# A gated mix of a state-space model and an MLP: W1 sums made twice, a longer-running scan, full-size bias rows, another load order

## The chip, the cores and the metric

The kernel runs on one core of one Trainium2 chip. The time is that of the device in microseconds (us); smaller is better. Eight runs of the kernel before have a median of 574.28 us (573.9 to 575.57). Engines are named as the profile names them: PE multiplies matrices, PEld is its weight loader, DVE works on vectors, ACT applies functions, POOL and SP mostly issue transfers here.

## The reference

For `x` of 2048 rows by 1024 columns, all in bfloat16:

```
g = sigmoid((x * gate_w).sum(-1))
# a: state-space model, P = 1024 complex states
Bu = x @ B_bar.T                      # B_bar = ((Lam_bar-1)/Lam) * (B_re + 1j B_im)
h[t] = Lam_bar * h[t-1] + Bu[t]       # a scan over 2048 rows
a = 2 * Re(h @ C.T) + x * Dskip
# b: MLP
y = layernorm(x)
b = gelu(y @ w1 + b1) @ w2 + b2       # w1: 1024 x 3584, w2: 3584 x 1024
out = g * a + (1 - g) * b
```

## The kernel before, in words

**An order worked out ahead.** Every step is a task with an engine, a duration, a priority and the memory that it reads and writes (class `Graph`, L172). Before the program is written, `_schedule_once` (L225) plays the tasks through and fixes the order of each engine's instructions; `emit` (L347) then writes them out with a wait for each dependency on another engine. A low first number in a priority means early. At run time each engine takes its instructions strictly in this order, so a DVE or SP instruction that waits holds everything behind it on that engine. SP issues loads, POOL issues most stores.

**Products in seven parts.** All large products are done in groups that make four 128x512 result blocks from seven partial products instead of eight (class `SG`, L836; parts `p1` to `p7`). For this DVE makes sums and differences of operand blocks beforehand (`dve_tt`, L881). ACT copies intermediate PSUM banks (L846, L847, L854), and DVE or ACT evict the results. `mm` (L819) issues the 4 to 8 matmuls of one part, L828 those that start a bank and L830 those that add to it.

**Stages.** They follow each other on PE:

1. *Head, 0 to 26 us.* SP loads the first 128-row blocks of B (real, imaginary) and the first four of x. PE transposes them through PSUM (`t_x`, L641; `t_b`, L657); DVE copies x out, ACT copies B out. `tbank` gives PSUM banks 7 and 3 in turn. A transpose `cst_T` (L683) turns the small vectors into columns; a long chain of small DVE operations for the scan's tables starts from it.
2. *Projection `bu`, to about 124 us.* x times B. A narrow product (`z_gate`, L1024; into bank 7) gives for each row the gate's sum and the row sum for the layernorm. `z_move` (L1043) takes both through DRAM, once, after the second half. POOL and DVE make the layernorm; its result goes to DRAM and comes back transposed (`xn_load`, L1191).
3. *MLP, about 120 to 470 us.* Blocks of 1024 rows (c) and half of the 3584 hidden columns (Fh), in the order (Fh, c) = (0,0), (0,1), (1,1), (1,0). Each has an `m` part (times W1, GELU; seven groups) and a `b` part (times W2; four groups). `w1_prep` (L1219) brings one 256-column piece of W1 into one of four slots. On its first use the piece comes raw, DVE makes four sums from it (L1236 to L1239) and POOL stores piece and sums (`scr_w1`, L1241); on the second use this is loaded back (L1225). Each `b` group writes its result times (1-g) to DRAM (`scr_ac`), for Fh=1 by adding (L1366). For Fh=0, b2 is added by one more matmul in `p1` and in `p5`: its stationary operand is the first row, or the first two, of a constant tile `STG` (`v_one`, `v_sgn`, L690), its moving operand one or two rows of b2 in the region `B2B` (L1182, loaded at L1557).
4. *Scan, spread over stages 2 and 3.* Sixteen units (`ssm`, L1120): two groups of 512 states by eight pieces of 256 rows. Each loads from `scr_u`, does four wide products, four combinations, eight scans and a few small corrections on DVE (L1142 to L1173), and stores to `scr_h`. Its priority is 50, after that of the MLP's work (10). It has three slots in the region `SSM`, and its tables in `TABR`.
5. *Output `y`, about 470 to 567 us.* Eight groups, each for 256 rows: the state times C. `y_load` (L1417) loads the state (`H0`), the partial sums of the MLP (`AV`), x and the skip vector (`DB`), and DVE adds x * Dskip (`xd`, `xa`, L1433 and L1434, priority 52). The order of the row blocks is `YORD` (L1381). The arena regions of `H0`, `AV`, `XV`, `DB` are shared with the buffers of earlier stages, which decides when their loads can start. Before, the first two states lie in `SSM` and the first four partial sums in `TABR`: both become free when the scan is done. `y_load(0)` and `y_load(1)` stand before the last `b` group.

Of the kernel before, what the change touches and what calls it, by code (L numbers as in the profile page):

```python
# [419 lines left out]
def build(nc, A_x, A_Lambda_re, A_Lambda_im, A_B_re, A_B_im, A_C_re, A_C_im, A_log_dt, A_Dskip,  # L420
# [6 lines left out]
    CH = 512  # L427
# [18 lines left out]
    with es:  # L446
# [194 lines left out]
        def t_x(k, prio):  # L641
            bk = tbank()
            v = XNAT[k]

            def em(e, k=k, bk=bk):
                ins = None
                base = XNAT[k].ap
                for dt in range(DT):
                    src = AR.v(XOFF(k) + dt * 256, [(1, 128)]).ap
                    ins = e.transpose(V(PS16[bk], dt * 128, [(1, 128)]), src, V(IDENT, 0, [(1, 128)]))  # L650
                return ins
            g.add("pe", 0.06 * DT, prio, em, reads=[v, b_ident], writes=[b_ps[bk]], name="xT_T%d" % k)
            o = AR.v(xqo(0, 0) + k * 256, [(512, DT), (1, 128)])
            first_e.append(g.add("dve", 0.65, prio, lambda e: e.tensor_copy(o.ap, V(PS16[bk], 0, [(128, DT), (1, 128)])),
                                 reads=[b_ps[bk]], writes=[o, b_ps[bk]], name="xT_e%d" % k))

        def t_b(pt, prio):  # L657
            s = pt % 4
            for ri in range(2):
                bk = tbank()  # L660

                def em(e, ri=ri, bk=bk):
                    ins = None
                    for dt in range(DT):
                        src = AR.v(RX + s * 4096 + ri * 2048 + dt * 256, [(1, 128)]).ap
                        ins = e.transpose(V(PS16[bk], dt * 128, [(1, 128)]), src, V(IDENT, 0, [(1, 128)]))
                    return ins
                g.add("pe", 0.06 * DT, prio, em, reads=[BN[pt], b_ident], writes=[b_ps[bk]], name="bT%d.%d" % (pt, ri))
                o = AR.v(bqo(pt, 2 * ri), [(1, D)])
                first_a.append(g.add("act", c_act(D), prio, lambda e, o=o, bk=bk: e.activation(o.ap, V(PS16[bk], 0, [(1, D)]), AF.Copy),  # L670
                                     reads=[b_ps[bk]], writes=[o, b_ps[bk]], name="bTe%d.%d" % (pt, ri)))

        load_b(0, (-0.95, 0))
# [5 lines left out]
        for k in range(4):  # L679
            t_x(k, (-0.8, k))  # L680
        t_b(0, (-0.79, 0))
        bk0 = tbank()
        g.add("pe", 0.06, (-0.75, 0),  # L683
              lambda e: e.transpose(V(PS16[bk0], 0, [(1, NROW)]), V(STG, 0, [(1, 128)], npart=NROW), V(IDENT, 0, [(1, NROW)], npart=NROW)),
              reads=[b_stg, b_ident], writes=[b_ps[bk0]], name="cst_T", extra=[g.tasks[-2]])
        g.add("pool", 0.4, P0,
              lambda e: e.affine_select(V(STG, 0, [(1, 128)], npart=2), V(ONESF, 0, [(1, 128)], npart=2), [[0, 128]], ALU.is_equal, -1.0,
                                        base=0, channel_multiplier=1),
              reads=[b_ones], writes=[b_stg], name="signs").slack = 4.0
        v_one = View(V(STG, 0, [(1, 128)], npart=1), [b_stg])  # L690
        v_sgn = View(V(STG, 0, [(1, 128)], npart=2), [b_stg])
# [324 lines left out]
        b_zs = B("zs")  # L1016
# [26 lines left out]
        def z_move():  # L1043
            prio = (1.0, seq[0])

            def em_st(e):
                return [e.dma_start(out=ZS[r].rearrange("(c t) -> c t", c=NCH), in_=bass.AP(AR.h[F32], r * zrow + ZR // 4, [[32 * zrow, NCH], [1, CH]])) for r in range(2)]
            g.dma(prio, em_st, 2 * L * 4, sem("d_zst", True), reads=[zr], writes=[b_zs], name="zst", ndma=2, q="pool").slack = 0.5

            def em_ld(e):  # L1050
                return [e.dma_start(out=C(("Z", "SUM")[r], 0, NTT), in_=bass.AP(ZS.tensor, ZS.offset + r * L, [[1, 128], [128, NTT]]), allow_slow_non_contiguous=True) for r in range(2)]
            g.dma(prio, em_ld, 2 * L * 4, sem("d_zl"), reads=[b_zs], writes=[bc("Z%d" % k) for k in range(NTT)] + [bc("SUM%d" % k) for k in range(NTT)], name="zl", ndma=2)
# [15 lines left out]
        for c in range(2):  # L1068
            if c == 1:
                z_gate(0)  # L1070
            for pt in range(2):
                bu_plain(pt, c)
# [4 lines left out]
        for n, (pt, pr) in enumerate(order):  # L1077
            if pt not in summed:
                b_sums(pt, seq[0] - 1)
                summed.add(pt)  # L1080
            if (pt, pr) == (0, 1):
                z_gate(1)
                z_move()
                x_sums(1, seq[0])
            cur = bu_group(pt, pr)
            cur.p1()
            if prev is not None:
                prev.p7()
            cur.p5()
            cur.p6()  # L1090
            cur.p2()
            cur.p3()
            if prev is not None:
                prev.p4()
                opt = order[n - 1][0]
                if order[n - 1][1] == 1 and opt < 3:
                    bT_dma(opt + 5)
            prev = cur
# [21 lines left out]
        def ssm(pg, q):  # L1120
            s = nxt("sb", NSB)
            so, MA, MB = SB0 + s * 4096, TM0, TM0 + 4096
# [59 lines left out]
        v_b2l = AR.v(B2B, [(1, 512)], npart=1)  # L1182
        v_b2r = AR.v(B2B + 1024, [(1, 512)], npart=2)
# [35 lines left out]
        def w1_prep(j, first, q, ex=()):  # L1219
            s = nxt("w1", 4)  # L1220
            o0 = W1R + s * 7168
            w1slot[j] = o0
            if not first:
                o = AR.v(o0, [(1, 3584)])
                g.dma((10.0, q - 7), lambda e: e.dma_start(out=o.ap, in_=W1S[j]), 128 * 7168, ssem("w1", s), reads=[b_w1s[j]], writes=[o], name="w1l%d" % j, extra=ex)  # L1225
                return
            o = AR.v(o0, [(256, DT), (1, 256)])
            g.dma((10.0, q - 7), lambda e: e.dma_start(out=o.ap, in_=B_w1[:, j * 256:(j + 1) * 256].rearrange("(dt p) f -> p dt f", p=128)),
                  D * 256 * 2, ssem("w1", s), writes=[o], name="w1_%d" % j, bw=DMA_BW_512, extra=ex)

            def raw(fo, dh, dt=BF16):
                return AR.v(o0 + (dh * 1024 + fo * 128) * 2, [(256, 4), (1, 128)], dt)

            def sq(i):
                return AR.v(o0 + 4096 + i * 1024, [(128, 4), (1, 128)], FP16)
            dve_tt("w1a%d" % j, q, sq(0), raw(1, 0), raw(1, 1), ALU.add, 512)  # L1236
            dve_tt("w1b%d" % j, q, sq(1), sq(0), raw(0, 0), ALU.subtract, 512)
            dve_tt("w1c%d" % j, q, sq(2), raw(0, 0), raw(1, 0), ALU.subtract, 512)
            dve_tt("w1d%d" % j, q, raw(1, 0, FP16), raw(0, 1), sq(1), ALU.subtract, 512)  # L1239
            ov = AR.v(o0, [(1, 3584)])  # L1240
            g.dma((10.0, q), lambda e: e.dma_start(out=W1S[j], in_=ov.ap), 128 * 7168, ssem("w1s", s, True), reads=[ov], writes=[b_w1s[j]], name="w1s%d" % j, q="pool")  # L1241
# [85 lines left out]
        def b_group(Fh, c, tp):  # L1327
# [8 lines left out]
            if Fh == 0:  # L1336

                st["A11"], mv["B11"] = st["A11"] + [v_one], mv["B11"] + [v_b2l]
# [33 lines left out]
        H0 = [SSM, SSM + 8192] + [HT + 8192 * i for i in range(4)] + [SSM, SSM + 8192]  # L1372
        YR = HT + 49152
        AV = [TABR + 4096 * i for i in range(4)] + [YR + 4096 * i for i in range(4)]
        XV = [SSM + 16384, YR + 16384, YR + 18432, HT + 43008, HT + 45056]
        DB = SSM + 18432
# [4 lines left out]
        YORD = (4, 5, 6, 7, 0, 1, 2, 3)  # L1381
# [35 lines left out]
        def y_load(yi):  # L1417
# [3 lines left out]
            g.dma((52.0, yi), lambda e: e.dma_start(out=o.ap, in_=HS[qb]), 2 * UE * 128 * 2, ssem("hg", yi), reads=[b_hs[pg][qb] for pg in range(PG)], writes=[o], name="hg%d" % yi,  # L1421
                  extra=pe_last if yi > 2 else ())
            if yi == 0:
                g.dma((51.0, 0), lambda e: e.dma_start(out=v_db.ap, in_=bass.AP(A_Dskip.tensor, A_Dskip.offset, [[0, 128], [1, D]])), 128 * D * 2, sem("d_dskb"), writes=[v_db], name="dskb")
            for t in range(2):
# [3 lines left out]
                xi = 0 if n < 4 else 1 + n % 4  # L1429
# [3 lines left out]
                g.add("dve", c_tt16(D), (52.0, n), lambda e, xv=xv: e.tensor_tensor(xv.ap, xv.ap, v_db.ap, ALU.mult), reads=[xv, v_db], writes=[xv], name="xd%d" % k)  # L1433
                g.add("dve", c_dve(D), (52.0, n, 1), lambda e, xv=xv, av=av, k=k: e.scalar_tensor_tensor(av.ap, xv.ap, C("G", k), av.ap, ALU.mult, ALU.add),  # L1434
                      reads=[xv, av, bc("G")], writes=[av], name="xa%d" % k)

        def y_group(yi):
# [5 lines left out]
            su, s5 = AR.v(YU[yi % 2], [(1, 512)], F32), AR.v(AO + 16384, [(1, 512)], F32)  # L1443
# [23 lines left out]
        for (kind, Fh, c) in blocks:  # L1467
            if kind == "m":
                for j in range(NP2):
                    w1order.append((Fh * NP2 + j, (Fh, c) in ((0, 0), (1, 1))))  # L1470
# [37 lines left out]
        for n, it in enumerate(flat):  # L1508
# [4 lines left out]
            if (kind, Fh, c, x) == ("b", 1, 0, 3):  # L1513
                y_load(0)
                y_load(1)
# [39 lines left out]
            if n == 0:  # L1555
                def em_b2(e):
                    return [e.dma_start(out=AR.v(B2B, [(1, D)], npart=1).ap, in_=bass.AP(B_b2.tensor, B_b2.offset, [[0, 1], [1, D]])),  # L1557
                            e.dma_start(out=AR.v(B2B + 1024, [(1, 512)], npart=1, p0=1).ap, in_=bass.AP(B_b2.tensor, B_b2.offset, [[0, 1], [1, 512]]))]
                g.dma((40.0, 0), em_b2, 4096, sem("d_b2b"), writes=[v_b2l, v_b2r], name="b2b", ndma=2)
# [6 lines left out]
            if last_of_block:  # L1566
                if nit is None:
                    prev.p4()
                else:
# [13 lines left out]
                    else:  # L1583
# [5 lines left out]
                        prev.p4()  # L1589
                    prev = None  # L1590
# [53 lines left out]
```

## Time and profile before

| what | value |
|---|---|
| median of 8 runs | 574.28 us |
| the profiled execution's own time | 575.57 us |
| its span, first to last instruction | 573.8 us |
| mean granted TensorE clock | 0.998 |
| PE busy | 554.8 us, 2617 matmuls |
| DVE busy | 511.6 us, 865 instructions |
| ACT, POOL busy | 279.7 us, 99.5 us |
| moved by DMA | 134.5 MB, 234 GB/s |

All times are from one execution. In its lists a group of instructions has its line in the kernel, engine and operation, then the shapes of the operands and how often it ran. "Idle before" is the time in which the engine did nothing just ahead of an instruction, and the arrow names what ended this. Matmuls overlap in the records: one lasts 0.38 us, but the next starts 0.216 us after it.

### The profile page before, as it was taken

How to read it: one execution, taken by the hardware profiler on the slowest of the kernel's cores; microseconds unless marked ns; L12 is line 12 of the kernel's file. 1: busy time of each engine (PE TensorE's matmuls, PEld its weight loads, DVE VectorE, ACT ScalarE, POOL GpSimd, SP SyncE). 2: the span in 40 equal slices, each digit the busy share in tenths (PEclk: the TensorE clock that was granted, in tenths of full speed). 3: DMA queues.
4: the chain of work that ended last, by engine and by line, in shares of the span. 5: the costliest groups of instructions: out<-in, count | busy, mean ns of one | idle time of the engine just before them, and what ended most of it. 6: DMA issues, size and time to landing. Idle time of an engine off the chain costs nothing.

```text
span 573.8 us, 7480 instructions
## 1 busy us (share of the span) xinstructions
PE 554.8 (97%) x2617; PEld 249.3 (43%) x2617; DVE 511.6 (89%) x865; ACT 279.7 (49%) x465; POOL 99.5 (17%) x159
## 2 busy tenths in 40 slices
PE   4999999999999999999999999999999999999994
PEld 3444444444334444444434444444444444444442
DVE  2899899999999999999999999999995868998652
ACT  2978989666652247752226673236663322111110
POOL 0024766630101010001211000210000210011000
PEclk9999999999999999999999999999999999999999
DMA  9994999988994766413778998899569999777501
GB/s 269 246 276 99 285 268 295 339 282 268 368 282 121 257 243 224 157 37 111 254 293 295 342 322 181 210 278 265 186 145 244 318 304 287 245 245 271 174 37 55
DMA packets 116675, 134.50 MB, mean 234 GB/s; under 512 B 70548, under 2 KB 92565, under 8 KB 115614
## 3 DMA queue, kind: packets, MB, share of 16 engines
q1 hardware_dynamic: 102548, 79.72, 49.9%
q0 software_dynamic: 13952, 54.29, 29.1%
q8 instruction: 20, 0.33, 0.2%
q14 instruction: 17, 0.14, 0.1%
q10 hardware_dynamic: 138, 0.02, 0.0%
HBM read 63.48 MB, written 54.80 MB: 206 GB/s over the span
## 4 chain that ended last, share of the span: by engine, by line
PE 85%; DVE 9%; ACT 2%; issue 1%; DMA 1%; SPq 0%; DVEq 0%
PE ps L830 59%; PE ps L828 25%; DVE ar L882 3%; DVE ar L1142 2%; DVE ar L1275 2%; DVE ar L1156 1%; DVE ar L1145 1%; DMA ar<-in_A_x_dram 1%; ACT ar L670 1%; PE ps L1033 1%; PE ps L650 1%; DVE ar L1357 0%; ACT ar L912 0%; ACT L720 0%; ACT L1104 0%
## 5 line engine op out<-in xcount | busy, mean ns | idle before, releaser
L830 PE MATMUL ps<-ar 128*128 128x512 f16 (+1 forms) x1720 | 391.8, 379 | 2.2 <-DVE ar L1357 1.0
L830 PEld LDWEIGHTS ps<-ar 128*128 128x128 f16 (+1 forms) x1720 | 166.3, 98 | 207.4 <-issue 4.4
L828 PE MATMUL ps<-ar 128*128 128x512 bf16 (+1 forms) x752 | 183.7, 379 | 1.0 <-DVE ar L882 0.8
L882 DVE TENSOR_TENSOR ar<-ar 128x512 f16<-128x512 bf16 (+7 forms) x216 | 139.5, 683 | 8.1 <-PE ps L828 3.4
L828 PEld LDWEIGHTS ps<-ar 128*128 128x128 bf16 (+1 forms) x752 | 72.7, 98 | 90.1 <-DVE ar L882 3.5
L1156 DVE TENSOR_TENSOR_SCAN ar<-cst,init,ar 128x256 bf16<-128x256 f32 x128 | 87.8, 733 | 0.4
L846 ACT ACTIVATE ar<-ps 128x512 f32<-128x512 f32 x100 | 58.9, 593 | 48.1 <-PE ps L828 33.0
L1142 DVE TENSOR_TENSOR ar<-ar 128x2048 bf16<-128x2048 bf16 x64 | 77.1, 1216 | 0.0
L854 ACT ACTIVATE ps<-ps 128x512 f32<-128x512 f32 x66 | 38.5, 583 | 71.7 <-PE ps L828 71.5
L1271 ACT ACTIVATE ar<-ps,cst 128x512 bf16<-128x512 f32 x56 | 38.4, 687 | 25.7 <-PE ps L830 25.0
L847 ACT ACTIVATE ar<-ps,cst 128x512 f32<-128x512 f32 x32 | 22.0, 687 | 56.6 <-PE ps L828 35.7
L1354 ACT ACTIVATE ar<-ps,cst 128x512 f32<-128x512 f32 x32 | 22.0, 687 | 46.1 <-PE ps L830 46.1
L1277 ACT ACTIVATE ar<-ar,cst 128x512 bf16<-128x512 f32 x56 | 40.0, 715 | 8.9 <-DVE ar L1275 8.8
L1145 DVE TENSOR_TENSOR ar<-ar 128x1024 bf16<-128x1024 bf16 x64 | 42.2, 683 | 0.2
L1275 DVE TENSOR_TENSOR ar<-ps,ar 128x512 f32<-128x512 f32 x56 | 38.2, 682 | 2.8 <-PE ps L830 2.4
L897 POOL DMA_DIRECT2D scr_u<-ar x32 | 25.1, 786 | 52.1 <-ACT ar L912 17.8
L1357 DVE SCALAR_TENSOR_TENSOR ar<-ps,cst,ar 128x512 f32<-128x512 f32 x32 | 23.9, 746 | 11.2 <-PE ps L830 11.1
L1455 DVE SCALAR_TENSOR_TENSOR ar<-ps,cst,ar 128x512 bf16<-128x512 f32 x32 | 23.7, 746 | 9.7 <-PE ps L830 9.6
L1366 POOL DMA_DIRECT2D scr_ac<-ar x16 | 13.8, 881 | 81.2 <-issue 32.9
L1364 POOL DMA_DIRECT2D scr_ac<-ar x16 | 8.5, 534 | 100.6 <-DVE ar L882 47.7
L1462 POOL DMA_DIRECT2D out_dram<-ar x14 | 7.6, 546 | 83.4 <-DVE ar L1455 83.4
L1174 POOL DMA_DIRECT2D scr_h<-ar x16 | 9.6, 602 | 66.9 <-DVE ar L1145 66.7
(105 smaller groups left out, 262.0 us busy)
## 6 DMA issues: line engine op xcount, KB each, us to landing
scr_ac<-ar POOLq DMA_DIRECT2D x32, 512.0 KB, 7.6
scr_w<-ar POOLq DMA_DIRECT2D x14, 896.0 KB, 6.6
ar<-scr_w SPq DMA_DIRECT2D x14, 896.0 KB, 6.1
ar<-in_A_x_dram SPq DMA_DIRECT2D x32, 256.0 KB, 5.1
scr_u<-ar POOLq DMA_DIRECT2D x32, 256.0 KB, 5.0
ar<-scr_u SPq DMA_DIRECT2D x16, 512.0 KB, 5.9
scr_h<-ar POOLq DMA_DIRECT2D x16, 512.0 KB, 7.1
ar<-scr_ac SPq DMA_DIRECT2D x16, 512.0 KB, 7.4
```

The costliest lines, as they stand in the source:

```text
L828: ins = e.matmul(V(PS[bk], 0, [(1, n)]), st[i].ap, mv[i].ap, start=(i == 0), stop=(i == K - 1))
L830: ins = e.matmul(V(PS[bk], 0, [(1, n)]), st[i].ap, mv[i].ap, start=False, stop=(i == K - 1), skip_group_check=True)
L846: return e.activation(o.ap, V(PS[bk], 0, [(1, 512)]), AF.Copy)
L854: g.add("act", c_act(512), (pb[0], q - 2), lambda e: e.activation(V(PS[b], 0, [(1, 512)]), V(PS[a], 0, [(1, 512)]), AF.Copy), reads=[b_ps[ ...
L882: g.add("dve", c_tt16(n), (pb[0], q), lambda e: e.tensor_tensor(o.ap, a.ap, b.ap, op), reads=[a, b], writes=[o], name=nm, extra=ex).slack ...
L897: g.dma((1.0, q), lambda e: e.dma_start(out=US[pt // 4, :, 4 * pr:4 * pr + 4, r0:r0 + T], in_=evv.ap), 2 * 128 * CH * 2, ssem("us", 2 * ks ...
L1142: g.add("dve", c_tt16(UE), pri(i), lambda e: e.tensor_tensor(o.ap, a.ap, tbl.ap, ALU.mult), reads=[a, tbl], writes=[o], name=nm + tag)
L1145: g.add("dve", c_tt16(UE // 2), pri(i), lambda e: e.tensor_tensor(o.ap, a.ap, b.ap, op), reads=[a, b], writes=[o], name=nm + tag)
L1156: lambda e, pt=pt, ri=ri, vin=vin, go=go: e.tensor_tensor_scan(go.ap, Cb("R", pt, T), vin.ap, V(INIT, pt * 2 + ri, [(1, 1)]), ALU.mult, AL ...
L1271: g.add("act", c_act(512, ap_operands=1), (10.0, q + 1), lambda e: e.activation(o.ap, V(PS[bk], 0, [(1, 512)]), AF.Gelu_apprx_tanh, bias=C ...
L1275: g.add("dve", c_dve(512), (10.0, q - 2), lambda e: e.tensor_tensor(sv.ap, V(PS[bk], 0, [(1, 512)]), sv.ap, ALU.add), reads=[b_ps[bk], sv] ...
L1277: g.add("act", c_act(512, psum=False, ap_operands=1), (10.0, q + 3), lambda e: e.activation(o.ap, sv.ap, AF.Gelu_apprx_tanh, bias=C("B1", ...
```

## The change

- W1: both uses of the first half's seven pieces load them raw and make the four sums; they are not stored. The second half is as before.
- The scan gets a fourth slot: units 13 to 15 use slots 2 and 3 in turn, where slot 3 is `TABR + 4096`, in the first group's tables.
- Output stage: states, partial sums, x blocks and the skip vector have other places; the skip vector takes over `B2B`. The row blocks go in the order 4, 5, 6, 0, 1, 2, 3, 7. The loads for the first two groups, the first state aside, stand after the last `b` group. `xd` and `xa` have priority 49.
- b2: a POOL memset clears all 128 rows of `B2B`, the constant tile is filled over 128 rows, and the extra matmuls take 128-row operands.
- Head: x0, x1, B real, x2, x3, B imaginary are loaded and transposed in this order, through banks chosen by hand.
- The gate's sums go through DRAM in two halves.

The diff, cut:

```diff
-        load_b(0, (-0.95, 0))
+        def load_b0(ri, ap):
+            v = AR.v(RX + ri * 2048, [(1, D)])
+            g.dma((-0.9, 1.5 + 2 * ri), lambda e: e.dma_start(out=v.ap, in_=ap[0:128, :]), 128 * D * 2,
+                  sem("d_b0%d" % ri), writes=[v], name="bnat0.%d" % ri)
+
+        load_b0(0, A_B_re)
+        load_b0(1, A_B_im)
...
-        for k in range(4):
-            t_x(k, (-0.8, k))
-        t_b(0, (-0.79, 0))
-        bk0 = tbank()
+        t_x(0, (-0.8, 0), 7, [])
+        t_x(1, (-0.8, 1), 3, last_pe())
+        t_b(0, (-0.8, 2), (0,), (1, 2), last_pe())
+        t_x(2, (-0.8, 3), 0, last_pe())
+        t_x(3, (-0.8, 4), 7, last_pe())
+        t_b(0, (-0.79, 0), (1,), (1, 2), last_pe())
+        bk0 = 3
...
-              lambda e: e.affine_select(V(STG, 0, [(1, 128)], npart=2), V(ONESF, 0, [(1, 128)], npart=2), [[0, 128]], ALU.is_equal, -1.0,
+              lambda e: e.affine_select(V(STG, 0, [(1, 128)]), V(ONESF, 0, [(1, 128)]), [[0, 128]], ALU.is_equal, -1.0,
...
+                z_move(0)
...
-                z_move()
+                z_move(1)
...
-            s = nxt("sb", NSB)
-            so, MA, MB = SB0 + s * 4096, TM0, TM0 + 4096
+            un = pg * NQ + q
+            s = nxt("sb", NSB) if un < 13 else 2 + un % 2
+            so, MA, MB = (SB0 + s * 4096 if s < 3 else TABR + 4096), TM0, TM0 + 4096
...
-        v_b2l = AR.v(B2B, [(1, 512)], npart=1)
-        v_b2r = AR.v(B2B + 1024, [(1, 512)], npart=2)
+        v_b2l = AR.v(B2B, [(1, 512)])
+        v_b2r = AR.v(B2B + 1024, [(1, 512)])
+        v_b2 = AR.v(B2B, [(1, D)])
...
+            if j < NP2:
+                return
             ov = AR.v(o0, [(1, 3584)])
             g.dma((10.0, q), lambda e: e.dma_start(out=W1S[j], in_=ov.ap), 128 * 7168, ssem("w1s", s, True), reads=[ov], writes=[b_w1s[j]], name="w1s%d" % j, q="pool")
...
-                st["A11"], mv["B11"] = st["A11"] + [v_one], mv["B11"] + [v_b2l]
+                st["A11"], mv["B11"] = st["A11"] + [v_sgn], mv["B11"] + [v_b2l]
...
-        H0 = [SSM, SSM + 8192] + [HT + 8192 * i for i in range(4)] + [SSM, SSM + 8192]
+        H0 = [SSM] + [HT + 8192 * i for i in range(4)] + [SSM, HT, HT + 8192]
-        AV = [TABR + 4096 * i for i in range(4)] + [YR + 4096 * i for i in range(4)]
-        XV = [SSM + 16384, YR + 16384, YR + 18432, HT + 43008, HT + 45056]
-        DB = SSM + 18432
+        AV = [YR + 4096 * i for i in range(4)] + [AO + 2048, AO + 10240, TABR + 8192, TABR + 12288]
+        XV = [TABR, YR + 16384, YR + 18432, HT + 43008, HT + 45056]
+        DB = B2B
-        YORD = (4, 5, 6, 7, 0, 1, 2, 3)
+        YORD = (4, 5, 6, 0, 1, 2, 3, 7)
...
-                    w1order.append((Fh * NP2 + j, (Fh, c) in ((0, 0), (1, 1))))
+                    w1order.append((Fh * NP2 + j, (Fh, c) in ((0, 0), (0, 1), (1, 1))))
...
             if (kind, Fh, c, x) == ("b", 1, 0, 3):
-                y_load(0)
-                y_load(1)
+                y_load(0, ())
...
+                g.add("pool", 0.8, (39.0, 0), lambda e: e.memset(v_b2.ap, 0.0), writes=[v_b2], name="b2z")
                 g.dma((40.0, 0), em_b2, 4096, sem("d_b2b"), writes=[v_b2l, v_b2r], name="b2b", ndma=2)
...
+                        if nk == "y":
+                            y_load(0, (0, 1), False)
+                            y_load(1)
```

## The prediction

> **What bounds the kernel now.** I read first the page's busy table and slices, then the windows by stage, PE's waits, the chain that ended last, PE's and the weight loader's timelines around its gaps, then the built instruction order of both kernels.
>
> ```profile
> PE 554.8 (97%) x2617; PEld 249.3 (43%) x2617; DVE 511.6 (89%) x865; ACT 279.7 (49%) x465; POOL 99.5 (17%) x159
> ...
> PE   4999999999999999999999999999999999999994
> ...
> DVE  2899899999999999999999999999995868998652
> ```
>
> PE is the bound; DVE is as full until about slice 30 (430 us) and has air only after it. PE ends at 566.6: 6.8 us pass before its first instruction, 7.2 after its last, and 5.0 lie idle between (566.6 - 6.8 - 554.8). PE's timeline shows where:
>
> ```profile
> 6.77 3.71 PE L650 MATMUL ps<-ident,ar 128*128 128x128 bf16 x32 [6.77 <-DMA ar<-in_A_x_dram]
> ...
> 12.63 0.21 PE L684 MATMUL ps<-ident,stg 76*128 76x76 bf16 x1 [0.41 <-ACT ar L670]
> ...
> 24.00 1.89 PE L1033 MATMUL ps<-ar,gwc 128*2 128x512 bf16 x16 [1.43 <-DVE ar L768]
> ...
> 151.39 1.04 PE L828 MATMUL ps<-ar 128*128 128x512 f16 x4 [0.53 <-DVE ar L882]
> ...
> 299.18 4.28 PE L830 MATMUL ps<-ar 128*128 128x512 f16 x19 [1.02 <-DVE ar L1357]
> ```
>
> The bracket is idle time and what ended it. The other DVE waits over 0.2 are 0.23, 0.34, 0.23 and 0.31: 2.66 in all, at 145 to 161, 299, 324 to 331 and 430. There is also loss that no idle column shows. In the chain that ended last:
>
> ```profile
> 169.97 6.15 PE ps L830 x28
> 176.12 1.83 PE ps L828 x8
> ...
> 347.03 6.04 PE ps L830 x28
> ...
> 383.29 1.73 PE ps L828 x8
> ```
>
> The same 28 and 8 matmuls take 0.11 and 0.10 longer where a b2 row is mixed in (first W2 half) than where none is (second).
>
> **The change part by part.**
>
> *x first.* SP issues in order. Now B_re, B_im, x0 to x3; after: x0, x1, B_re, x2, x3, B_im, six transfers of the same size. So each slot keeps its landing and the tenants change. By the landing records the first two are in by 4.1, the others at 6.73, 7.27, 7.92, 8.59. Transposes of one block take 0.86 (1.71 for two). x0, x1 done by 5.8; B_re 6.75 to 7.6; x2 to 8.5; x3 to 9.35; B_im to 10.2; the constants' transpose 0.2. x3's copy (0.69) ends at 10.15, so the first projection matmul starts at about 10.4 instead of 12.67: **-2.3**. DVE's chain of constants starts after the same transpose, so DVE also gains 2.3. ACT's copies, which pace the chain from 14.6 to 21.5, follow B_im's, which moves by the same 2.2.
>
> *Bank rota.* The transposes of B alternate banks 7 and 3; six fixed banks at the head shift the rota by one. The gate matmul (bank 7) now waits for the copy of B block 3's real part (ended 22.46) and no longer its imaginary part (23.86). PE is done with transposes at 22.58, so the 1.43 gap closes: **-1.4**. Head for PE: **-3.7**.
>
> *b2 rows of full size.* Weight loader:
>
> ```profile
> 167.46 0.09 PEld L828 LDWEIGHTS ps<-ar,stg 1*128 1x128 bf16 x1 [0.42 <-issue]
> ...
> 169.58 0.09 PEld L828 LDWEIGHTS ps<-ar,stg 2*128 2x128 bf16 x1 [0.42 <-issue]
> ```
>
> The 1- and 2-row loads come late, and each costs 0.10 before and 0.11 after it. 16 x 0.21 = **-3.4** if a 128-row operand behaves as its neighbours. The Trainium skill, "TensorE: Matmul & The Clock Gate", LDWEIGHTS, speaks against it: loading time goes by columns, not by rows of the contraction; by that the sum has 0. The 0.09 here agrees with it about the load itself, but the spacing does not. "TensorEngine Tiling (Array Packing)", Key Properties, says that changing the array's tiling mode drains it, which would fit if one row counts as another mode; no record says so. I take the measured spacing, 3.4; the bounds are 0 and 3.4. New is a POOL memset of 128x1024 ahead of the two b2 loads on SP. The row near it (128x128, 205 ns) gives 0.2 to 1.6; I take 0.8. Behind it on SP is the first W2 quarter, issued at 130.1 when PE frees its place; the b2 loads went at 125.8, so 4 us cover it. On POOL, one store of u waits behind it; nobody needs that soon.
>
> *W1 sums twice.* Seven stores (0.55 each on POOL, 896 KB) and seven reloads go; seven raw loads of 512 KB come, and 28 sums:
>
> ```profile
> L882 DVE TENSOR_TENSOR ar<-ar 128x512 f16<-128x512 bf16 x66 | 26.1, 417 | 1.6 <-ACT ar L670 0.6 <-PE ps L828 0.5
> ```
>
> Back to back they are 0.34 to 0.41 apart: 28 x 0.357 = **+10.0 of DVE**, all in the stage 208 to 254, where DVE has 1.7 us free. It is hidden only by moving scan work out. The built order does: at the start of the second half's output block (345) 11.3 us less of the scan stands ahead on DVE than now. If that cover were gone, the 10 us would fall on PE. A W1 load is issued when a slot's matmuls end, two groups (12 us) ahead, and takes 6.4; SP waits ahead of these loads (a scan load behind a store of h, 7.1) end before PE frees the slot.
>
> *Gate sums moved in two halves.* Two more small stores on POOL (0.59 each, as the two now) and two more loads on SP. The first SP pair waits for its store and ACT's copy, at about 26; behind it stands a transpose of B that waits for PE until about 49 anyway. The layernorm chain starts earlier, PE never waited for it: 0.
>
> *DVE against PE.* At the sums that PE waited for (145 to 161 and 324 to 331), the new order has 0.3 to 3.1 us less DVE work ahead, mostly 0.65. That alone would end most of the 2.35 us of waits before 343. But PE, ahead by 3.7 + 3.4 + 2.35 = 9.45, would ask DVE to be 9.45 ahead too. DVE gets 2.3 from the head and 0.65 from the order: 2.95. The rest must come from its idle time, which between 26 and 343 is 9.8 us by the windows, for instance
>
> ```profile
> 168.00:208.00 40.00, 40.00 (x180) 17.03 (x181) 38.36 (x59) 12.00 (x18) 3.78 (x8) 1.00 0.61 191
> 254.00:294.00 40.00, 40.00 (x180) 16.90 (x179) 38.32 (x63) 12.05 (x18) 4.79 (x9) 1.00 0.55 191
> ```
>
> (third busy figure DVE.) These are short waits for PE's results (0.2 to 0.7), and shrink as PE runs ahead; but the order is fixed, and where both engines are full each waits sometimes. Gain by 343: 2.95 at worst, 9.45 at best; I take 3.55 of the 9.8, hence **-6.5**.
>
> *Scan into the output stage; y loads later.* DVE idles 14 us between 430 and 490, so the last scan unit, about 12.5 us, fits. The 0.31 at 430 goes (1.7 us less ahead): **-0.3**. y's partial sums now lie where W2 lay, and so do the second and third state: their loads start only as W2's last group frees them. From the second state's issue (457.8, PE's row) to the third's landing, 6.0 MB of loads and some 2.3 MB of partial-sum stores pass. These windows give the rate (last figures: DMA share, GB/s):
>
> ```profile
> 457.00:470.00 13.00, 13.00 (x62) 5.93 (x61) 10.42 (x15) 3.41 (x6) 2.58 (x3) 1.00 1.02 284
> 470.00:485.00 15.00, 15.00 (x71) 6.80 (x70) 10.75 (x14) 3.64 (x6) 1.43 (x2) 1.00 1.06 303
> ```
>
> 8.3 MB at 300 is 28 us: 485.5. It is needed at 493.2 (y2's sum, 0.7 ahead of PE at 493.9). x's block for y0's second row, issued at 468.4 behind a MB, lands at about 479 and must be there by 485.5 (3.2 us of DVE before PE's bank at 488.7). Six to eight us of cover; I charge **+0.3**. The order of blocks still ends with one whose outputs leave as now, so the 7.2 tail stays.
>
> Sum against the profiled execution: 573.8 - 6.5 - 0.3 + 0.3 = 567.3 span. That execution took 575.57, 1.8 more than its span; the median 574.28 is 0.5 more. Difference onto the median: **567.8**.
>
> **Rivals.**
> - *PE keeps it all:* DVE reclaims enough idle time: 574.3 - 9.75 = 564.5. For it: 9.8 us are idle. Against: they are spread over thirty-odd waits, some for ACT or POOL.
> - *DVE gives nothing back:* only its 2.95 passes, and 0.3: about 571.2. For it: DVE is 96 to 99% busy in most windows.
> - *Full-size rows gain nothing* (the page's rule holds): PE asks for 6.1; with DVE in between, some -5: 569.3.
> - *The output stage starves, slower:* the third state lands late. PE stalls if its 8.3 MB come below 234 GB/s (35.4 us), and the kernel is slower than before once the stall passes 6.5 us, below 198 GB/s. The window with the transposes of C, 427 to 440, ran at 195 (DMA share 0.95), and two of those transposes precede these loads on SP. Against: they are issued at 430, nearly 30 us earlier. Price 8 us: about 576.
>
> **How the numbers follow.** Forecast 0.46, PE keeps all 0.18, DVE holds 0.14, rows gain nothing 0.12, starved 0.10. The likeliest case has its own range of 565.8 to 570; for 8 in 10 I take 563.8 to 572.4, leaving out starvation and the edge of the best case. A change under 0.2% (1.15 us) cannot be told from none; a milder starvation would land there: faster 0.88, same 0.03, slower 0.09.
>
> **What would show it.** First projection matmul at 10.4 and no gap before the gate matmul; blocks with b2 at 6.04 and 1.73; 244 f16 sums of L882's kind in place of 216, with none of PE's waits in 208 to 254 over 0.3; PE's DVE waits in 145 to 331 under 1 us or DVE at 99%; DVE at 8 or more in slices 30 to 33; no PE wait for DVE at 470 to 495. I am wrong if the b2 spacing stays, if PE gains waits on DVE before 343 in place of the head's gain, or if the output stage shows waits for loads of h or of the partial sums.

## The result, and the profile after

Over 19 runs the changed kernel has a median of 572.2 us (567.15 to 580.97), the kernel before, over 56 runs, 575.24 us. The ratio is 0.9917, with a 95% interval of 0.9900 to 0.9935: faster by 0.8%, inside the predicted range of 563.8 to 572.4, but only 0.2 us inside its upper end and 4.4 us above the predicted 567.8. Five of the 19 runs lie at 567.15 to 568.04, at the predicted value. So the question is what the other runs lose. (Ratios leave out runs that are over 1.5% above the fastest of their kernel, while medians and ranges hold all; the profile of the changed kernel shown here is of such a run, 578.3 us with a span of 576.6.)

From the page of the changed kernel, busy times and slices:

```profile
PE 555.0 (96%) x2617; PEld 251.3 (44%) x2617; DVE 519.7 (90%) x893; ACT 279.4 (48%) x465; POOL 94.1 (16%) x155
...
PE   6999987899999999999999999999999999999995
...
DVE  4999885999999999999999999999998995999952
...
PEclk9999998899999999999999999999999999999998
```

DVE has 28 instructions and 8.1 us more (10.0 us were forecast), and fills slices 30 to 32 (counted from 0: 8, 9, 9 for 5, 8, 6), though not 33 (5 for 8). New are the holes of PE in slices 5 to 7, at 72 to 115 us, and of DVE in 5 and 6; the granted clock drops in slices 6 and 7. Line numbers differ between the kernels: L828, L830 and L882 of before are L839, L841 and L893 here, and others in the experiments. PE's timeline, the lines with the longer waits, with the idle time in brackets:

```profile
3.42 1.89 PE L649 MATMUL ps<-ident,ar 128*128 128x128 bf16 x16 [3.42 <-DMA ar<-in_A_x_dram]
6.11 1.03 PE L665 MATMUL ps<-ident,ar 128*128 128x128 bf16 x8 [0.80 <-DMA ar<-in_A_B_re_dram]
...
9.73 1.89 PE L839 MATMUL ps<-ar 128*128 128x512 bf16 x8 [0.28 <-DVE cst L704]
...
77.42 1.90 PE L841 MATMUL ps<-ar 128*128 128x512 bf16 x8 [2.02 <-ACT ar L857]
88.82 3.93 PE L841 MATMUL ps<-ar 128*128 128x512 f16 x16 [0.85 <-ACT ps L865]
97.81 3.52 PE L841 MATMUL ps<-ar 128*128 128x512 f16 x8 [2.47 <-ACT ps L865]
101.83 1.90 PE L841 MATMUL ps<-ar 128*128 128x512 bf16 x8 [0.51 <-ACT ar L857]
110.08 2.38 PE L841 MATMUL ps<-ar 128*128 128x512 bf16 x8 [2.03 <-ACT ar L857]
...
174.59 1.68 PE L839 MATMUL ps<-ar 128*128 128x512 f16 x7 [0.72 <-DVE ar L893]
...
302.65 4.28 PE L841 MATMUL ps<-ar 128*128 128x512 f16 x19 [0.38 <-DVE ar L1379]
```

The head came as forecast: the first projection matmul at 9.73 (forecast 10.4, before 12.67), and no gap ahead of the gate matmul. Then PE waits five times for ACT's copies of intermediate banks, where it never waited before. The waits between 55 and 125 us say what held ACT and DVE (the figures are total, times, longest):

```profile
DVE ar L893 <- DMA ar<-in_B_w_dram: 6.9, 1, 6.9
ACT ar L968 <- DMA scr_u<-ar: 5.1, 3, 2.8
PE ps L841 <- ACT ar L857: 4.6, 3, 2.0
...
DVE ar L893 <- DMA ar<-in_A_B_im_dram: 4.0, 2, 3.7
...
PE ps L841 <- ACT ps L865: 3.3, 2, 2.5
```

All are transfers: blocks of B that a DMA transposes, stores of u that give their buffers back, a piece of W1. None stands in this list of the kernel before.

The b2 rows did what was forecast. The chain that ended last has, for the first W2 half, the spacing that only the second had before (the first had 6.15 and 1.83), and the loader shows the 128-row operand like its neighbours:

```profile
176.49 6.04 PE ps L841 x28
182.53 1.73 PE ps L839 x8
```

```profile
169.18 1.39 PEld L839 LDWEIGHTS ps<-ar 128*128 128x128 bf16 x7
170.69 0.10 PEld L839 LDWEIGHTS ps<-ar,stg 128*128 128x128 bf16 x1
170.90 0.74 PEld L841 LDWEIGHTS ps<-ar 128*128 128x128 bf16 x4
```

To see where time goes, I compare the start of the same ACT or DVE instruction, one that follows PE directly, in two traces. This table gives the start minus that of the kernel before, in us; the head of the table has the time in the trace of before.

| kernel, own time of its profile | 26.0 gate copy | 67.7 u3 | 110.3 u7 | 160.7 GELU 6 | 339.0 GELU 13 | 463.9 last W2 | 508.0 y3 |
|---|---|---|---|---|---|---|---|
| changed, 578.3 | -4.25 | -4.26 | +7.76 | +6.48 | +3.03 | +2.98 | +3.12 |
| changed, again, 572.5 | -4.03 | -4.04 | -0.30 | +0.04 | -3.33 | -3.32 | -2.67 |
| b2 only, 573.45 | -1.19 | -1.01 | -1.13 | -0.92 | -3.69 | -3.62 | -2.12 |
| head only, 573.88 | -4.04 | -4.17 | -2.32 | -2.72 | -2.73 | -2.72 | -1.73 |
| head only, 584.39 | -4.89 | -5.02 | +8.97 | +8.55 | +8.55 | +8.56 | +8.76 |
| gate halves only, 585.5 | -1.09 | -1.06 | +6.00 | +10.19 | +9.82 | +9.89 | +9.86 |
| changed, gate in one piece, 571.0 | -3.39 | -3.48 | -3.39 | -4.34 | -6.06 | -5.93 | -4.24 |
| changed, old head, 586.6 | -1.07 | -1.00 | +11.60 | +15.04 | +11.10 | +11.22 | +11.50 |
| changed, old head, gate in one piece, 572.8 | -1.22 | -1.15 | -1.21 | -0.93 | -2.86 | -2.74 | -2.41 |
| changed, old head, stores held, 575.1 | -0.11 | -0.04 | +1.67 | +1.23 | -1.19 | -1.13 | -0.15 |
| changed, stores held, 572.6 | -3.34 | -3.35 | +0.26 | -1.43 | -3.09 | -2.97 | -2.85 |
| changed, W1 sums stored, 572.6 | -3.76 | -3.83 | -3.89 | -2.96 | -4.17 | -3.60 | -3.33 |
| b2 and W1, 596.5 | -0.72 | -0.65 | -0.71 | -0.35 | -3.17 | -2.92 | +21.36 |

The column at 67.7 is steady: -3.4 to -5.0 with the new head, 0 to -1.2 with the old one (the trace of before happened to get its first x late, at 6.77; with the old head the others start at 5.0 to 6.0). Most of the spread between the traces comes in by the next two columns, at 110.3 and 160.7; the other large loss is that of the last row, at the output.

### The profile page after: what moved, and what is told of

It is laid out like the page before. It is cut to its first block, busy times and chain, and to the rows that moved or that the text cites. A ratio compares the mean times of both kernels' runs of the same rounds, so it can differ in the third digit from the quotient of the medians.

```text
span 576.6 us, 7505 instructions
## 1 busy us (share of the span) xinstructions
PE 555.0 (96%) x2617; PEld 251.3 (44%) x2617; DVE 519.7 (90%) x893; ACT 279.4 (48%) x465; POOL 94.1 (16%) x155
## 4 chain that ended last, share of the span: by engine, by line
PE 79%; DMA 8%; DVE 8%; issue 2%; ACT 0%; SPq 0%; DVEq 0%; ACTq 0%
PE ps L841 54%; PE ps L839 24%; DMA ar<-in_B_w_dram 4%; DVE ar L893 3%; DMA ar<-in_A_B_im_dram 2%; DMA scr_u<-ar 2%; DVE ar L1297 1%; DVE ar L1160 1%; DMA ar<-in_A_B_re_dram 1%; PE ps L665 1%; PE ps L1044 1%; DVE ar L1163 0%; DVE ar L1174 0%; DVE ar L1019 0%; PE ps L649 0%
## 5 line engine op out<-in xcount | busy, mean ns | idle before, releaser
L841 PE MATMUL ps<-ar 128*128 128x512 f16 (+1 forms) x1720 | 394.7, 381 | 9.1 <-ACT ar L857 4.6
L841 PEld LDWEIGHTS ps<-ar 128*128 128x128 f16 (+1 forms) x1720 | 167.8, 98 | 216.9 <-ACT ar L857 7.8
L839 PE MATMUL ps<-ar 128*128 128x512 bf16 (+1 forms) x752 | 184.6, 380 | 1.5 <-DVE ar L893 1.2
L893 DVE TENSOR_TENSOR ar<-ar 128x512 f16<-128x512 bf16 (+7 forms) x244 | 150.7, 652 | 13.9 <-DMA ar<-in_B_w_dram 6.9
L839 PEld LDWEIGHTS ps<-ar 128*128 128x128 bf16 (+1 forms) x752 | 73.1, 98 | 91.5 <-DVE ar L893 3.7
L968 ACT ACTIVATE ar<-ps 128x512 bf16<-128x512 f32 x28 | 16.7, 596 | 10.4 <-DMA scr_u<-ar 5.1
```

Of the source, the lines that this page charges most:

```text
L839: ins = e.matmul(V(PS[bk], 0, [(1, n)]), st[i].ap, mv[i].ap, start=(i == 0), stop=(i == K - 1))
L841: ins = e.matmul(V(PS[bk], 0, [(1, n)]), st[i].ap, mv[i].ap, start=False, stop=(i == K - 1), skip_group_check=True)
L893: g.add("dve", c_tt16(n), (pb[0], q), lambda e: e.tensor_tensor(o.ap, a.ap, b.ap, op), reads=[a, b], writes=[o], name=nm, extra=ex).slack ...
```

## The experiments

Theory 1 was that the early head pushes transfers together at 60 to 115 us and loses its gain there. The rival was the gate part, which lets the layernorm, and so its stores, start earlier.

**The change again.**

> The changed kernel, unaltered, once more, because its profiled execution lost some 12 us between 75 and 115 us, where PE waited for ACT's copies, ACT for stores of u and DVE for W1 and for transposed blocks of B. Theory 1 (late transfers are an accident of an execution, not of the order): a profile of an undisturbed execution has under 1 us of PE waits between 60 and 120, keeps the head's 4.4 us there, and spans about 565.5. Theory 2 (the new order always collides there): waits of 5 us or more in the same place again, and a span over 570.

569.42 us (566.58 to 572.51, 6 runs), ratio 0.9895 [0.9858, 0.9933]. Its six runs fall into three at 566.6 to 567.7 and three at 571.2 to 572.5. The profile is of one of the latter. PE's waits between 60 and 120 us sum to 3.74, more than Theory 1's 1 us and less than Theory 2's 5, so neither theory holds as it stands. From PE's timeline:

```profile
78.51 1.90 PE L841 MATMUL ps<-ar 128*128 128x512 bf16 x8 [2.89 <-ACT ar L857]
103.71 1.90 PE L841 MATMUL ps<-ar 128*128 128x512 bf16 x8 [0.85 <-ACT ar L857]
127.78 3.63 PE L841 MATMUL ps<-ar 128*128 128x512 f16 x16 [1.45 <-ACT ps L865]
152.56 3.63 PE L841 MATMUL ps<-ar 128*128 128x512 f16 x16 [0.25 <-DVE ar L893]
168.23 1.69 PE L839 MATMUL ps<-ar 128*128 128x512 f16 x7 [0.72 <-DVE ar L893]
...
487.85 1.90 PE L839 MATMUL ps<-ar 128*128 128x512 bf16 x8 [0.55 <-DMA ar<-scr_h]
```

The wait at 78.5 comes after DVE stood 4.69 us for a transposed block of B. The one at 127.8 is of another kind: DVE has scan work ahead of the evictions there, and ACT waits 2.09 us for DVE. The last one, at the output, is for the third state.

**b2 rows alone.** The kernel before with

```diff
-                st["A11"], mv["B11"] = st["A11"] + [v_one], mv["B11"] + [v_b2l]
+                st["A11"], mv["B11"] = st["A11"] + [v_sgn], mv["B11"] + [v_b2l]
```

and the memset, the constant tile and the views of 128 rows.

> The kernel before with only the full-size b2 rows (memset, 128-row constant tile, 128-row operands). If the measured spacing is due to the 1- and 2-row operands: runs of 28 matmuls after a b2 row take 6.04 in place of 6.15, those of 8 take 1.73 in place of 1.83, and the span falls by up to 3.4 us, less what DVE takes back since its order is the old one: -1.5 to -3.4. If the rows' size does not matter: 0.

574.16 us (571.66 to 584.3, 22 runs), ratio 0.9974 [0.9957, 0.9991]. Between 160.7 and 339 the shift goes from -0.92 to -3.69, a gain of 2.8 where 16 operands at 0.20 would give 3.2. At the output 1.5 of it is lost again, in the old output stage. By the median the gain is 1.1 us, under the 1.5 to 3.4 that were expected.

**Head alone.** Loads, transposes and banks of the head on the kernel before.

```diff
-        load_b(0, (-0.95, 0))
+        load_b0(0, A_B_re)
+        load_b0(1, A_B_im)
...
-            t_x(k, (-0.8, k))
+        t_x(0, (-0.8, 0), 7, [])
+        t_x(1, (-0.8, 1), 3, last_pe())
```

> The kernel before with only the head's new order of loads, transposes and banks. By the prediction PE's first projection matmul starts 2.3 us earlier and the gate matmul 3.7 earlier; with DVE's order of the old kernel the time falls by 2 to 3.7 us. Theory: the earlier start alone brings on the late stores and transposes between 75 and 115 us; then its runs spread as those of the changed kernel do (6 us between lowest and upper quarter) and the median gains under 1 us. Rival: the spread has another cause; then all runs lie within 3 us and the gain stays.

582.62 us, from 573.88 to 595.13 over 22 runs; the kernel before on the same chip has 575.25. A head that is 3 us earlier makes the kernel 7 us longer in the median. Over the ten shortest runs alone the ratio is 1.0036 [1.0009, 1.0064]: still slower, by 2 us. The profile, of the best run, shows the head's 4.2 and a loss of 1.9 between 67.7 and 110.3, in which PE waits 1.62 us at 93.6.

**Gate in one piece.** The changed kernel with one store and one load of the gate's sums:

```diff
-                z_move(0)
...
-                z_move(1)
+                z_move()
```

> The changed kernel with the gate's sums moved in one piece after the second half, as before. If the earlier layernorm stores and the transposes that follow them cause the waits between 75 and 115 us: the runs draw together and the median falls by 2 to 5 us against the changed kernel, to about 567. If not: the same 572 with the same spread.

572.38 us (568.68 to 576.56, 19 runs), ratio 0.9939 [0.9916, 0.9962]. The expectation failed: the median didn't fall to 567, and the middle half of the runs spreads over 5.5 us, in the changed kernel over 5.9. Its best run (568.68) is even 1.5 to 2 us above the best runs of the changed kernel (567.15 and 566.58). So by the run times the gate halves cost the changed kernel nothing that can be told from zero. Its profile, of one run, is what the prediction forecast: no loss at 60 to 115, -6.06 at 339 (forecast -6.5). It then loses 1.8 at the output, in one wait:

```profile
484.55 1.90 PE L841 MATMUL ps<-ar 128*128 128x512 f16 x8 [1.60 <-DVE ar L1473]
```

DVE had stood 8.0 us for blocks of x in this stage. What makes this kernel's other runs up to 5.6 us longer than the profiled one was not profiled.

**Old head.** The changed kernel with the head of before.

> The change without its first part: x and B are loaded in the old order and the transposes keep the old banks, all else is as after the change. Theory 1 (the early head is what makes the transposed blocks of B and of the normalized x late between 60 and 115, so its gain comes back there): no waits of DVE on transposed B above 0.5 us, no waits of PE on copies of u, runs within 3 us of each other, and a time of 575.2 - 3.3 (b2 rows) - 2.4 (PE's waits for DVE before 343) - 0.3, or about 569.3, no slower than with the head. Theory 2 (the gate sums in halves do it, since they start the layernorm stores 6 us earlier, into the transposes): the lateness and the spread stay, with a time of 572 to 576. Theory 3 (the head is worth its 3.7 in the runs that go well): the best runs are 3 to 4 us above the best of the changed kernel (566.6).

587.4 us (586.57 to 588.6, 4 runs), ratio 1.022 [1.0186, 1.0255]: worse than the kernel before, and steadily so. Theory 1 as written falls: the early head isn't needed for the collision, the gate halves are enough. That is Theory 2, though the time goes far beyond its 572 to 576. SP's timeline shows it, here of before:

```profile
65.74 5.25 SPq L1062 DMA_TRANSPOSE ar<-in_A_B_im_dram  x2
74.52 5.05 SPq L1197 DMA_TRANSPOSE ar<-scr_xn  x2
```

and here with the old head and gate halves:

```profile
62.29 17.33 SPq L1065 DMA_TRANSPOSE ar<-in_A_B_im_dram  x2
79.80 9.02 SPq L1205 DMA_TRANSPOSE ar<-scr_xn  x2
```

Issuing the last two transposes of B takes 17.3 us in place of 5.3, and they land 23.6 and 14.0 us after their issue, before 7.3 and 5.9. The stores of normalized x left at 61.5 to 72.5 us, in the kernel before at 66 to 80. DVE waits, then ACT's copies, then PE:

```profile
DVE ar L881 <- DMA ar<-in_A_B_im_dram: 12.6, 1, 12.6
PE ps L829 <- ACT ar L845: 8.5, 2, 8.3
```

**Old head and gate in one piece.**

> The old head and the gate sums moved in one piece; b2 rows, W1 sums twice and the output stage as after the change. Theory 1: as the kernel before in its first 120 us, so neither lateness nor spread, about 569.3. Theory 2: the same here, and 3 us or more better than the run that has only the old head. If the gate halves are worth something by an earlier layernorm chain: slower than that run.

572.92 us (570.77 to 580.0, 10 runs), ratio 0.9964 [0.9936, 0.9992]. Taking the halves away is worth 14.5 us here. Its first 120 us are those of the kernel before. It stays 3.6 us above the 569.3 that Theory 1 expected: PE waits 1.26 us for ACT at 126.8, and 3.1 us for DVE in six places (before 2.7 in six).

**b2 and W1 twice, old output stage.**

```diff
-                    w1order.append((Fh * NP2 + j, (Fh, c) in ((0, 0), (1, 1))))
+                    w1order.append((Fh * NP2 + j, (Fh, c) in ((0, 0), (0, 1), (1, 1))))
...
+            if j < NP2:
+                return
```

> The kernel before with full-size b2 rows and the W1 sums made twice, with the old buffers and block order of the output stage. The built order still defers 8.5 us of scan past the second half's first sums (11.3 after the change). Theory (10.0 us more of DVE lie beside other work as long as scan can be deferred): within 1.5 us of b2 rows alone (574.2), with the two DVE waits at 145 to 161 smaller. Rival (the 10 us need the new output stage as their cover): PE waits for DVE between 343 and 495, and the time is 578 to 584.

596.08 us (593.74 to 596.6, 4 runs), ratio 1.0356 [1.0322, 1.0390]. The rival was right that the old output stage doesn't hide the 10 us, though the loss is larger than its 578 to 584, and PE waits for a load, not for DVE. Up to 464 nothing is lost (-2.92). But the scan ends at 458.5 where it ended at 430, and the state that lies in the scan's own memory can't be loaded before. SP's timeline of the loads of h, first of before, then of this run, and PE's timeline of this run:

```profile
442.14 16.08 SPq L1421 DMA_DIRECT2D ar<-scr_h  x2
```

```profile
476.58 0.33 SPq L1423 DMA_DIRECT2D ar<-scr_h  x1
```

```profile
457.74 7.72 PE L829 MATMUL ps<-ar 128*128 128x512 f16 x34
487.45 5.78 PE L827 MATMUL ps<-ar 128*128 128x512 bf16 x16 [21.99 <-DMA ar<-scr_h]
```

The last store of h goes out at 464.3, takes 12.3 us, and only then the load is issued. The kernel with the new places and block order (the run before this one; it differs from this in them, in the order and priority of the output stage's loads and sums, and in the scan's fourth slot) has 572.92. So this part of the change is worth 23 us to a kernel that makes the W1 sums twice.

**W1 sums stored.** The changed kernel with the first half's sums stored and loaded again.

> After the change, but the first half of W1's sums is stored and loaded again as before: 28 sums (10.0 us of DVE) fewer, seven stores and seven loads of 128 KB in place of seven loads of 512 KB. Theory (the second making is hidden): the same time as the whole change, 567 to 572, within 1 us at equal luck in the first 120 us. Rival (DVE, not PE, sets the pace up to 343): 2 to 5 us faster than the whole change, 563 to 567. Second rival (the stores and their reloads cost more than the sums): 1 to 3 us slower.

573.88 us (570.7 to 578.34, 10 runs), ratio 0.9975 [0.9945, 1.0004]. Ten us less for DVE make nothing faster: the second making is hidden. It is 1.7 slower than the changed kernel's median, as the second rival had it, but the ranges lie over each other. Head and gate halves are both in this kernel, and its profile shows no loss between 67.7 and 110.3 (-3.83 to -3.89): with both, the collision comes in some executions only.

**Stores held, old head.** If the stores of normalized x are what holds the transposes up, then holding the stores must undo it:

```diff
+                hold = [t for t in g.tasks if t.name == "bs4_%d" % (5 + c)] if c < 2 else []
...
-                      reads=[xv, bc("RSTD" + s), bc("NMR" + s)], writes=[o], name="ln_norm%d" % k)
+                      reads=[xv, bc("RSTD" + s), bc("NMR" + s)], writes=[o], name="ln_norm%d" % k, extra=hold)
```

> The run with the old head and the gate sums in halves (587.4), with one edit: the first four normalized blocks of x are made after the sums of transposed B block 5, the next four after those of block 6, so that their stores leave some 6 us later. Theory (stores of normalized x that leave while B's last blocks are being transposed hold those transposes up, and through them DVE, the copies and PE): DVE's wait of 12.6 us for B falls under 1 us, no wait of PE over 1 us between 60 and 115, and the time comes to that of the old head with the old gate sums, 572 to 574. Rival (the transposes are late for another reason, such as their own start or the loads of u): the wait stays, 583 to 588. Second rival (held stores make the transposes of x late instead): DVE waits for normalized x between 85 and 125, 576 to 582.

574.69 us (572.02 to 576.44, 10 runs), ratio 0.9965 [0.9938, 0.9992], against 587.4. The stores left at 73.5 to 86.8; DVE's wait for B is gone. The waits between 55 and 125 us:

```profile
DVE ar L967 <- DMA scr_u<-ar: 2.6, 2, 1.6
ACT ar L956 <- DMA scr_u<-ar: 1.9, 1, 1.9
PE ps L829 <- ACT ps L853: 1.9, 1, 1.9
```

Not all is undone: three of B's last transposes, issued at 61.5, 63.3 and 70.6, still land after 13.1, 13.2 and 9.0 us (before 8.2, 7.3 and 5.9), though the first of the held stores leaves only at 73.5, and stores of u are late now. So holding the stores back ends DVE's wait, but the stores are not all that slows the transposes.

**Stores held, new head.** The same edit on the changed kernel.

> The changed kernel with the same edit: stores of normalized x held behind the sums of B blocks 5 and 6. Theory: no wait of DVE for B (4.7 and 6.9 us in the two profiles of the changed kernel), the head's 4.4 us kept until 115, and every run like the best ones of the changed kernel, 566 to 569, faster than it by 2 to 4 us. Rival (the lateness wasn't what spread the runs): 569 to 573 as before the edit. Second rival (the head starts so early that the transposes of x collide instead): 570 to 575 with waits at 85 to 125.

570.18 us (568.65 to 572.58, 4 runs), ratio 0.9886 [0.9850, 0.9923]. The wait for B is gone, but the theory's 566 to 569 isn't reached: the time is that of the rival, 569 to 573. PE loses 2.1 at 102.6, behind a copy for which ACT waited 2.26 us for DVE; DVE had worked without a pause since it waited 2.22 us for a store of u at 65.0. PE loses another 1.36 at 168 for DVE. The kernel beats the kernel before; against the changed kernel (0.9917) the intervals overlap, and four runs don't show whether the long ones are gone. So holding the stores mends the old head's kernel, and isn't shown to mend the changed one.

**Gate halves alone** on the kernel before.

> The kernel before with one part of the change: the gate sums moved in two halves. Theory: the halves alone do the damage seen with the old head, by 7 to 14 us, so 582 to 589, with DVE waiting 5 to 13 us for transposed B near 75. Rival (it takes more than the halves, such as the other memory places of the rest of the change): 575 to 577.

584.8 us (577.74 to 595.42, 10 runs), ratio 1.0111 [1.0076, 1.0146] over the six shortest. One part of the change, costed at 0, does 9 us of damage by itself in the median, and 6 us over those six. Its waits between 55 and 125:

```profile
DVE ar L882 <- DMA ar<-in_A_B_im_dram: 7.8, 2, 7.0
PE ps L830 <- ACT ar L846: 4.9, 4, 1.9
ACT ar L957 <- DMA scr_u<-ar: 4.2, 2, 3.6
```

**Head alone, a longer run.**

> A second look at the early head alone, whose runs lay between 573.9 and 595.1 while its one profile was of the best of them. Theory (in its slow executions the transposes of B or of the normalized x are late, as with the gate halves): DVE waits 3 us or more for transposed blocks between 60 and 125, and PE's shift against the kernel before turns from -4 to a loss there. Rival (the output stage starves, as with the old output buffers and deferred scan): PE keeps its 2.7 until 465 and then waits for loads of h. If this execution is a good one (574 to 576), the slow ones stay unexplained.

584.39 us. This execution was a long one, and PE stands still once:

```profile
90.08 1.03 PE L840 MATMUL ps<-ar 128*128 128x512 f16 x4
102.64 5.85 PE L842 MATMUL ps<-ar 128*128 128x512 f16 x16 [11.53 <-ACT ps L866]
```

Here no transposed block is waited for. The stores of u are late, by

```profile
ACT ar L969 <- DMA scr_u<-ar: 12.3, 2, 10.5
DVE ar L980 <- DMA scr_u<-ar: 11.7, 1, 11.7
PE ps L842 <- ACT ps L866: 11.5, 1, 11.5
```

while four transposes of normalized x are under way, issued from 72.6 to 107.0, which land 17.4, 25.0, 14.7 and 9.4 us after their issue (before 6.3, 9.1, 5.7 and 7.9). Four stores of u, issued from 78.1 to 84.8, take 18.9 to 21.6 us to land. It looks like the same collision from its other side. The windows of before and of this run (granted clock, DMA share, GB/s at the end):

```profile
90.00:105.00 15.00, 14.89 (x70) 6.60 (x69) 14.96 (x28) 13.83 (x26) 11.18 (x16) 1.00 1.13 316
```

```profile
90.00:105.00 15.00, 3.47 (x12) 1.18 (x10) 4.46 (x10) 6.17 (x12) 2.87 (x4) 0.62 1.20 168
```

The DMA engines are as busy and move half. The theory in its present form: transposes and plain stores that are in flight together can slow each other, and whichever the next engine needs first is late. The head and the gate halves each move one against the other. Being in flight together isn't enough: in the kernel before the two overlap as well, at 66 to 86 and at 88 to 98 us, without a wait of DVE or ACT for them.

Left open: why the early head, with the gate in one piece, spreads over 21 us on the kernel before and over 8 us in the changed one. They differ in b2, W1's stores and the output; of these only the first stores of W1's sums (one at 82.4 us in the long run, which took 19.9 us to land) fall into the window. That they are the cause wasn't tried on that pair; with the gate halves in it, the changed kernel with these stores put back ("W1 sums stored") spreads over 7.6 us, not 21.

## Why the prediction was right, and where not

- **Head, -3.7: right at its place, kept to 110 us in two traces of seven.** Over the profiles, the seven with the new head stand at -3.96 at 26 us in the mean, the seven with the old one (before among them, at 0) at -0.77: a gain of 3.2. The step counted the head's own transfers, but not that six transposed B blocks, their successors and the stores of u follow from it 3 to 5 us earlier, among other transfers.
- **Gate sums in halves, 0: the reason failed, the size only in part.** The cover named for it was PE's ("PE never waited for it"). What the earlier layernorm triggers was left out: sixteen stores of 256 KB, of which the first eight leave 3 to 12 us earlier (with the halves alone at 61.5 to 72.7, before at 66.0 to 80.0), among the last transposes of B. Price on the kernel before: 584.8 against 575.6, 9 us; in the changed kernel with the old head, 14.5 us. With the new head beside them, three profiles lose 0 to 12 us between 67.7 and 110.3 (from about -4 to between -3.9 and +7.8), yet the changed kernel's median is the same without the halves (572.2 and 572.38). There the 0 came true by luck, as far as the runs show: its reason names none of these transfers.
- **b2 rows, -3.4: right.** 6.04 and 1.73 as forecast, 2.8 measured and 3.2 by the spacing (0.20 apiece; the prediction took 0.21). That only columns count fits the load itself (0.09 and 0.10), and would have missed the spacing.
- **W1 sums twice, +10.0 hidden: right, for a reason that was stated only in half.** DVE's sums take 11.2 more (150.7 for 139.5). No wait of PE above 0.21 appears between 208 and 254. But "if that cover were gone, the 10 us would fall on PE" is wrong in place and size: with the old output stage the scan is still deferred, and the price is 22 us in one wait for the state.
- **DVE against PE, -6.5 by 343: right in the one profile with the new head where the collision stays away and the W1 sums are made twice** (-6.06 with the gate in one piece; some 0.8 of it is the late first x in the trace of before), -3.3 in the repeated run. DVE waits of PE at 145 to 331 were to be under 1 us; they are 1.9 in the repeated run, and its 1.45 for ACT at 127.8 were not foreseen (1.26 at 126.8 with the old head and the gate in one piece).
- **Output, +0.3 for late loads: mis-sized.** From 464 to 508 the lead over the kernel before shrinks by 0.7 (change again), by 1.7 (gate in one piece) and by 0.1 (the 578.3 us execution, where PE was late anyway). DVE stood 6.5 to 8.0 us for x there (before 1.8), and that held PE up by 1.6 with the gate in one piece. In the repeated run it was the state, as the forecast had it: from the second state's issue to the third's landing took 33.2 us (454.6 to 487.8) where 28 were reckoned, so the cover of six to eight us was used up and PE waited 0.55, the prediction's own sign of being wrong. The old output stage loses too (1.5 with the b2 rows alone), so not all of this belongs to the later loads.
- **Sum.** 567.8 is what five of 19 runs do, and three of the six in the repeat. None of these was profiled, so it isn't shown that they get there by the forecast's terms. Of the other runs two were profiled: they lost 12.0 and 3.7 us between 67.7 and 110.3, to late transposes of B, stores of u and, in the first, a load of W1. That this is what sets the median 4.4 us above the forecast is likely, not shown: neither the gate in one piece nor the held stores brought the median to 567. That the time lies inside the range owes something to the range's width, which was meant for DVE and the output stage and held nothing for late transfers at 60 to 115 us.

## What to carry to other kernels

A step that PE never waits for is not free for that reason alone: list the transfers that it releases, and what else is on the DMA engines at their new time, here the DMA transposes. When two parts of a change each move a stream of transfers, test them apart and together, since here each alone cost 7 to 9 us in the median, and the whole change, with both in it, gained. And look at the spread of the runs, not only at the median: here the head alone took it to 21 us, and its first profile was of the best run, which shows little of the loss.

## What the hardware did that was not expected

**Transposes and stores.** The records of single packets show which transfers lose. In one microsecond without a packet of a store (before, 67 to 68 us), 907 packets of 256 bytes, those of the transposes, take 18 ns each, 232 GB/s in all. At 90 to 105 us, beside stores, such a packet takes 29 ns in the mean in the kernel before, and 62 ns in the long run of the head alone: most still take 18 ns, but 16% take over 100 (before 1%). There they take up 210 us of the DMA engines' time in place of 105 for about as many packets (3412 and 3638), and the number of 4 KB store packets falls from 571 to 187. The Trainium skill, "Advanced Engine Details and Errata", X-Bar Transpose (TRN2), has transposes as fast as regular transfers. It doesn't speak of stores beside them, for which these windows have 168 GB/s in the long run and 316 before; whether it holds for transposes alone no run here shows. Why the two hurt each other, and why only in some executions, no run here shows.

**A stall costs twice.** After PE stood for 11.53 us its next 16 matmuls took 5.85 in place of 3.63: 2.2 us more, at a granted clock of 0.50 from 102.6 to 107.2 us (1.00 from 12 to 93 and from 107.3 to 575). After 8.27 us with the old head, 8 took 3.59 in place of 1.90. "TensorE: Matmul & The Clock Gate", in its table on why this matters, warns of gaps over about 3 us. These traces have no such sharp edge: 2.47 us were enough in the changed kernel (97.81: 8 in 3.52, at a granted clock of 0.50), and 2.91 cost nothing with the gate halves alone (8 in 1.90 after it).
